# A transformer block on one core: phi's block matrix spread on chip, folds on 120 rows throughout, two folds in idle banks, modulation loaded ahead of the second x tile

## The chip, the core and the metric

The kernel runs on one core of a Trainium2 chip. A core has five engines with a queue of instructions each: TensorE (PE in the profile, with its weight loads as PEld), VectorE (DVE), ScalarE (ACT), GpSimd (POOL) and SyncE (SP), which here issues transfers. They share an on-chip memory of 128 partitions (SBUF), and PE writes its products into eight banks of a second one (PSUM). The metric is the device time of one execution in microseconds (us); three runs were taken and their median counts.

## The reference, cut to what matters

The input x has 2048 tokens of 640 features. All is 32-bit floating point.

```
mod = silu(c) @ w_mod                      # six rows of 640: sa, ca, ga, sb, cb, gb
h = layernorm(x) * (1 + ca) + sa
q, k, v = h @ wqkv                         # 32 heads of 20
pq, pk = q @ w_phi, k @ w_phi              # per head, 20x20
phi = concat(softmax(p), softmax(-p))      # per head
kv = phi_k^T v;  z = sum_s phi_k
o = (phi_q kv) / (phi_q z + 1e-6)
x = x + ga * (o @ wo)
h = layernorm(x) * (1 + cb) + sb
x = x + gb * (relu(h @ w1 + b1)^2 @ w2 + b2)
```

## The kernel before, in words

Tokens go in 16 tiles of 128, loaded two at a time (x0, x1 and so on: `load_x(j)`). A matrix product of full precision is made from three fast ones: each operand is split into a high part (ScalarE copies it to the type fp32r) and a low part (VectorE subtracts, `lo`, line 88). So most operands cost one step on ScalarE and one on VectorE after they are made.

The change lies in the prologue, up to the first tiles. Its work is this:

- *Warm-up.* `WARM` products of a tile of ones (line 563) run before any data has landed.
- *Folds.* Since phi is linear per head, w_phi is multiplied into the K and Q weights once. `fold(nm, d)` (line 246) makes one of five 128-row chunks: six products, five with 120 columns (six heads of 20 each) and one with 40 (the last two heads). The stationary operand is a piece of the raw weights, transposed on the host, with the six heads' 120 features on the partitions; the moving one is a slice of `bd_t`, the block matrix of w_phi with 640 columns, zero off the blocks. The last group has two heads, so its operands have 40 rows. The result lies in a pair of PSUM banks (`pj`, tag "pj": four banks, so two pairs that folds use in turn), from which `split` copies it out, two halves on ScalarE and two on VectorE.
- *Statistics.* `stats` (line 495) takes the mean and variance of an x tile on VectorE and a power on GpSimd; `scale` (line 511) normalizes both token tiles on ScalarE.
- *Modulation.* `mod_rows2(d)` (line 520) multiplies silu(c) with one fifth of the columns for sa and ca (`wm`), `mod_sb` copies the result to SBUF (`msb`, ScalarE), `mod_cols2` transposes it (line 538) and sums it into columns on VectorE (`cols_a`). `out0` then scales the transposed x by these columns into `hT` and splits it. The transposed x lies in halves of the three banks `kvp`, which are otherwise first used later, for phi_k^T v.
- *First K products.* `k_step(d)` adds chunk d to the K products of both token tiles (`pk`), which fill all four "pj" banks over five steps. `to_sb` copies them out (`k`), and `do_q` then starts the Q products (`pq`) in the same banks.
- *V weights.* `v_hi` and `v_lo` split the raw V weights (`rawv` to `wv`).

In this part the order on all five engines is that of the code (`manual_schedule` from line 195). SP issues all loads from one queue in the order of the code. After it a scheduler, and then orders by hand, set the rest: for all tile pairs K, V, Q, phi and the sums over tokens; then the normalized outputs, `wo` and the second layer norm; then the two large products of the last layers (`up` and `acc`), some two fifths of the chain of waits.

## Time and profile before

| | |
|---|---|
| median of 3 runs | 802.65 us (800.93 to 805.67) |
| profiled execution: span | 799.8 us; its own device time is not on the page |
| median run less that span | 2.85 us |
| PE busy | 786.2 us (98%) |
| VectorE, ScalarE busy | 580.0 us (73%), 443.7 us (55%) |
| start of the first fold | 6.43 us |
| start of the first product with Q weights (pq) | 39.46 us |

Times in the profile are us from the first instruction, durations of single instructions ns. In a row of the order of time stand start, duration, engine, line, operation, tiles as out<-in, shape and count; in brackets how long the engine had been idle and what released it. Rows of equal instructions that follow each other are merged. PE's ends are modelled, since products overlap: the spacing of starts tells more than durations. A product of 32-bit operands is two passes and counts twice.

### The profile page before, as it was taken

Reading aid. Unit: us, or ns where it says so; the run is one execution under the profiler, and the core shown is the slowest. Engines: PE = TensorE matmul, PEld = TensorE weight load, DVE = VectorE, ACT = ScalarE, POOL = GpSimd, SP = SyncE. Lnnn points to the kernel's source line nnn. Section 1 sums busy time; section 2 is a strip of 40 time slices with the busy share of each in tenths; the row PEclk is TensorE's granted clock in tenths of the full one; section 3 lists DMA queues with packets and bytes.
Section 4 is the critical chain, followed back from the end, with each engine's and each line's share of the span. In section 5 each row is a group of like instructions: output and inputs, shape, how many; then the busy total and the mean of one; then the engine's idle time right before and its main releaser. Section 6 shows DMA issues by size and latency. Waiting matters only on the chain.

```text
span 799.8 us, 15255 instructions
## 1 busy us (share of the span) xinstructions
PE 786.2 (98%) x5983; PEld 750.7 (94%) x5983; DVE 580.0 (73%) x1046; ACT 443.7 (55%) x988; POOL 127.8 (16%) x259
## 2 busy tenths in 40 slices
PE   9999999999999999999999999999999999999997
PEld 8899999999999878898899999989999999999997
DVE  4499889999788688993546666765857566675756
ACT  4667675576753355555777736455454545536431
POOL 3001021010000114331100000121131313212110
PEclk9999999999999999999999999999999999999999
DMA  9713326423120243321347355896575848557360
GB/s 330 289 35 128 115 83 203 148 84 116 67 100 1 80 168 132 116 83 67 116 150 240 122 197 210 283 302 220 181 215 171 252 145 268 168 184 225 104 187 34
DMA packets 50816, 126.30 MB, mean 158 GB/s; under 512 B 5872, under 2 KB 7152, under 8 KB 50744
## 3 DMA queue, kind: packets, MB, share of 16 engines
q1 hardware_dynamic: 33688, 84.32, 30.8%
q0 software_dynamic: 14752, 35.76, 15.3%
q10 hardware_dynamic: 2304, 5.24, 1.7%
q8 instruction: 47, 0.77, 0.4%
q14 instruction: 25, 0.20, 0.1%
HBM read 95.32 MB, written 29.88 MB: 157 GB/s over the span
## 4 chain that ended last, share of the span: by engine, by line
PE 80%; DVE 9%; ACT 4%; DMA 3%; POOL 2%; issue 1%; ACTq 0%; POOLq 0%; DVEq 0%
PE up L78 20%; PE acc L78 15%; PE pk L78 8%; PE pq L78 7%; PE pv L78 7%; PE pwo L78 7%; PE acc3x L78 4%; PE kvp L421 2%; DMA ring_c<-td_c 2%; DVE dn L790 2%; DVE scr L788 2%; PE te L829 2%; DMA ring_a<-td_a 1%; PE tb L340 1%; PE ta L340 1%
## 5 line engine op out<-in xcount | busy, mean ns | idle before, releaser
L78 PE MATMUL up<-h,w 128*128 128x256 f32 x1640 | 208.9, 279 | 0.4 <-ACT ft L1149 0.4
L78 PEld LDWEIGHTS up<-h,w 128*128 128x128 f32 x1640 | 197.8, 188 | 2.0 <-ACT ft L1149 1.8
L1149 ACT ACTIVATE ft<-up,b_t 128x256 f32<-128x256 f32 x104 | 49.0, 471 | 111.0 <-PE up L78 110.6
L78 PE MATMUL acc<-w,ra 128*128 128x384 f32 x452 | 98.7, 337 | 0.2
L78 PE MATMUL pwo<-wo,ot 128*128 128x256 f32 (+3 forms) x512 | 83.1, 315 | 0.1
L1150 DVE TENSOR_TENSOR ft<-ft 128x256 f32<-128x256 f32 x104 | 44.0, 423 | 52.9 <-ACT ft L1149 52.1
L78 PE MATMUL pk<-wk,hT 128*128 128x384 f32 (+1 forms) x480 | 77.3, 312 | 0.9 <-ACT hT L352 0.9
L78 PEld LDWEIGHTS pwo<-wo,ot 128*128 128x128 f32 (+1 forms) x512 | 75.7, 188 | 1.9 <-ACT ot L866 0.4
L78 PEld LDWEIGHTS acc<-w,ra 128*128 128x128 f32 x452 | 73.0, 188 | 2.8 <-DVE ra L88 1.7
L78 PE MATMUL pq<-wq,hT 128*128 128x384 f32 (+1 forms) x480 | 75.0, 311 | 0.4 <-ACT k L397 0.4
L78 PE MATMUL pv<-wv,hT 128*128 128x384 f32 (+1 forms) x480 | 75.2, 309 | 0.0
L78 PEld LDWEIGHTS pk<-wk,hT 128*128 128x128 f32 x480 | 71.7, 188 | 2.7 <-ACT hT L352 1.1
L78 PEld LDWEIGHTS pq<-wq,hT 128*128 128x128 f32 x480 | 70.7, 188 | 1.5 <-ACT k L397 0.9
L78 PEld LDWEIGHTS pv<-wv,hT 128*128 128x128 f32 x480 | 70.6, 188 | 0.4
L88 DVE TENSOR_TENSOR ra<-ft,ra 128x384 fp32r<-128x384 f32 (+2 forms) x86 | 36.8, 449 | 30.9 <-ACT ra L1173 17.6
L88 DVE TENSOR_TENSOR h<-hfb,h 128x256 fp32r<-128x256 f32 x40 | 17.0, 425 | 48.1 <-ACT h L352 48.0
L1173 ACT ACTIVATE ra<-ft 128x384 fp32r<-128x384 f32 x48 | 25.2, 526 | 29.2 <-DVE ft L1150 28.0
L78 PE MATMUL acc3x<-w,ra 128*128 128x256 f32 x248 | 41.3, 279 | 0.0
L1255 POOL DMA_DIRECT2D ring_c<-td_c x34 | 18.5, 544 | 139.4 <-PE acc L78 113.1
L78 PEld LDWEIGHTS acc3x<-w,ra 128*128 128x128 f32 x248 | 38.4, 188 | 0.4 <-DVE y L1312 0.2
L792 POOL TENSOR_TENSOR dn<-dn,rs_q 128x64 f32<-128x64 f32 x16 | 14.0, 875 | 128.0 <-DVE dn L790 128.0
L1164 DVE TENSOR_TENSOR ft<-ft 128x128 f32<-128x128 f32 x136 | 33.3, 286 | 1.2
(241 smaller groups left out, 1424.2 us busy)
## 6 DMA issues: line engine op xcount, KB each, us to landing
ring_c<-td_c POOLq DMA_DIRECT2D x34, 384.0 KB, 4.1
ring_a<-td_a POOLq DMA_DIRECT2D x34, 384.0 KB, 4.9
ring_b<-td_b POOLq DMA_DIRECT2D x34, 256.0 KB, 3.5
esp<-eq SPq DMA_DIRECT2D x12, 640.0 KB, 2.9
el<-esp SPq DMA_DIRECT2D x12, 640.0 KB, 3.9
rw<-in_w SPq DMA_DIRECT2D x23, 320.0 KB, 3.8
wm<-in_w_mod SPq DMA_DIRECT2D x20, 320.0 KB, 4.0
xb<-in_x SPq DMA_DIRECT2D x8, 640.0 KB, 4.0
```

Of the source, the lines that this page charges most:

```text
L78: nc.tensor.matmul(o, a, b, start=first and i == 0, stop=last and i == len(terms) - 1, skip_group_check=skip,)
L88: (eng or nc.vector).tensor_tensor(out_lo, full, hi.bitcast(F32), op=ALU.subtract)
L340: nc.tensor.transpose(p[:, i * P : (i + 1) * P], xn[:, i, d * P : (d + 1) * P], ident)
L421: nc.tensor.matmul(kvp[64 * c : 64 * c + 64, g // 4, a : a + 2 * n].rearrange("p (s n) -> p s n", s=2), v[:, u], e[:, :, o : o + n], start ...
L788: nc.vector.tensor_tensor(z, flat(ET[t]), flat(zb), op=ALU.mult)
L790: nc.vector.tensor_reduce(dn.rearrange("p s h -> p (s h)"), heads(z), axis=AX.X, op=ALU.add)
L829: nc.tensor.transpose(p[:m, a : a + P], EU[2 * j + i][:, b : b + m], ident)
L1149: nc.scalar.activation(r, p, AF.Relu, bias=b1_t[:, f : f + 1])
L1150: nc.vector.tensor_tensor(r, r, r, op=ALU.mult)
L1164: nc.vector.tensor_tensor(t[:, o], t[:, a], t[:, b], op=op)
L1173: nc.scalar.activation(a[:, 0, :3], t[:, :3], AF.Copy)
L1255: nc.gpsimd.dma_start(RING[j, n, r], TD[n][r].bitcast(F32R))
```

## The change

Six things, all in the prologue:

- `WARM` is 11 in place of 14.
- The host passes w_phi as 120x120 values (56 KB, all blocks side by side by their place within a group) in place of the 128x640 matrix (320 KB). On chip, GpSimd makes a 120x6 pattern of ones (`own`, a memset and two selects), and VectorE multiplies the two, spread over each other, into `bd_t` (two instructions). This stands ahead of VectorE's other work.
- The last group of every fold has 120 rows too. Its 80 more rows of raw weights are set to zero by a VectorE memset, before the load of the 40 real rows, which moves behind the first chunk's load. `bd_t` is zero there.
- The folds of Q chunks 0 and 3 write to two banks of `kvp` (`side_banks`) in place of a "pj" pair.
- The five loads of modulation weights go out together, ahead of the second x tile's. The modulation products of chunks 3 and 4 are made together, a step earlier, and their transposes too.
- The statistics of x1 and its scaling each move one step of `k_step` back; four K folds and not three stand ahead of x0's statistics, and two Q folds ahead of its scaling.

On PE, from the last product of the K folds through the first Q folds, before (foldk and foldq with 0 and 1 are the two banks of a "pj" pair):

```order
L256 MATMUL foldk_1_302<-bd_t,raw_k_129 128x40
L256 MATMUL foldq_0_316<-bd_t,raw_q_138 128x120 x3
L256 MATMUL foldq_1_317<-bd_t,raw_q_138 128x120 x2
L256 MATMUL foldq_1_317<-bd_t,raw_q_140 128x40
L256 MATMUL foldq_0_329<-bd_t,raw_q_138 128x120 x3
```

and after:

```order
L275 MATMUL foldk_1_307<-bd_t,raw_k_133 128x40
L275 MATMUL kvp<-bd_t,raw_q_143 128x120 x5
L275 MATMUL kvp<-bd_t,raw_q_145 128x40
L275 MATMUL foldq_0_330<-bd_t,raw_q_143 128x120 x3
L275 MATMUL foldq_1_331<-bd_t,raw_q_143 128x120 x2
```

The first Q fold goes to kvp's banks, and the second takes the pair that the first had.

On PE, around the last Q fold, before (kvp<-ident,xb are transposes of x, kvp<-ident,msb those of the modulation, mrow its products):

```order
L538 MATMUL kvp<-ident,msb_369 128x128
L256 MATMUL foldq_0_387<-bd_t,raw_q_140 128x120 x3
L256 MATMUL foldq_1_388<-bd_t,raw_q_140 128x120 x2
L256 MATMUL foldq_1_388<-bd_t,raw_q_140 128x40
L527 MATMUL mrow_399<-wm_149,cs 32x128 x10
L340 MATMUL kvp<-ident,xb_136 128x128 x6
L538 MATMUL kvp<-ident,msb_414 128x128
L527 MATMUL mrow_434<-wm_153,cs 32x128 x10
```

and after:

```order
L548 MATMUL mrow_364<-wm_153,cs 32x128 x10
L359 MATMUL kvp<-ident,xb_141 128x128 x2
L275 MATMUL foldq_0_384<-bd_t,raw_q_145 128x120 x3
L275 MATMUL foldq_1_385<-bd_t,raw_q_145 128x120 x2
L275 MATMUL foldq_1_385<-bd_t,raw_q_145 128x40
L561 MATMUL kvp<-ident,msb_381 128x128
L548 MATMUL mrow_398<-wm_155,cs 32x128 x10
L359 MATMUL kvp<-ident,xb_141 128x128 x8
L561 MATMUL kvp<-ident,msb_413 128x128
L548 MATMUL mrow_435<-wm_157,cs 32x128 x10
```

The first modulation transpose stands behind the fifth Q fold now, and only two transposes of x stand ahead of that fold, eight behind it.

On ScalarE, around the scaling of x1 (xb<-xb), before:

```order
L351 ACTIVATE hfa_3_506<-kvp,cols_a 128x256
L352 ACTIVATE hT_216<-hfa_3_506 128x256
L534 ACTIVATE msb_533<-mrow_510,plus 128x128
L513 ACTIVATE xb_151<-xb_151,nba_493,sqa_492 128x640 x2
L351 ACTIVATE hfa_4_539<-kvp,cols_a 128x256
L352 ACTIVATE hT_216<-hfa_4_539 128x256
L605 ACTIVATE wv_567<-rawv_159 128x640
L397 ACTIVATE k_570<-pk_0_424 128x384
```

and after:

```order
L370 ACTIVATE hfa_3_507<-kvp,cols_a 128x256
L371 ACTIVATE hT_224<-hfa_3_507 128x256
L370 ACTIVATE hfa_4_537<-kvp,cols_a 128x256
L371 ACTIVATE hT_224<-hfa_4_537 128x256
L532 ACTIVATE xb_163<-xb_163,nba_526,sqa_525 128x640 x2
L627 ACTIVATE wv_567<-rawv_165 128x640
L416 ACTIVATE k_570<-pk_0_425 128x384
L416 ACTIVATE k_570<-pk_1_426 128x256
```

The scaling has moved behind the last hT and stands directly ahead of the V weights and the copies of pk. On VectorE x1's statistics stand behind the fourth hT's low part, where they stood behind the third's.

The diff, cut:

```diff
...
-WARM = 14
+WARM = 11
...
 
     ones = const.tile([P, P], F32, name="ones")
     nc.gpsimd.memset(ones, 1.0)
+
+    bdc = row("s3", "bdc")
+    own = bdc[:120, P : P + 6]
+    nc.gpsimd.memset(own, 1.0)
+    nc.gpsimd.affine_select(out=own, in_=own, compare_op=ALU.is_ge, fill=0.0, base=0,
+                            pattern=[[-DH, 6]], channel_multiplier=1)
+    nc.gpsimd.affine_select(out=own, in_=own, compare_op=ALU.is_ge, fill=0.0, base=DH - 1,
+                            pattern=[[DH, 6]], channel_multiplier=-1)
     ident = const.tile([P, P], F32, name="ident")
     make_identity(nc, ident)
     neg = const.tile([P, P], F32R, name="neg")
...
     first.__enter__()
 
     nc.sync.dma_start(c_t, c)
+    nc.sync.dma_start(bdc[:120, :120], bd)
     bd_t = row("s4", "bd_t")
-    nc.sync.dma_start(bd_t, bd)
     raw, WM, RV, XB = {}, {}, {}, {}
 
     def load_raw(nm, w5, w1):
         raw[nm] = [tok2("w", f"raw_{nm}{i}") for i in range(3)]
-        nc.sync.dma_start(raw[nm][2][:40, 1], w1)
+        nc.vector.memset(raw[nm][2][:, 1], 0.0)
         for d in range(NC):
             nc.sync.dma_start(raw[nm][d // 2][:, d % 2], w5[d * P : (d + 1) * P])
+            if d == 0:
+                nc.sync.dma_start(raw[nm][2][:40, 1], w1)
 
     def load_x(j):
         XB[j] = tok2(f"x{j % 2}", f"xb{j}")
...
     load_raw("k", wk5, wk1)
     load_x(0)
     load_raw("q", wq5, wq1)
-    for d in range(2):
+    for d in range(NC):
         load_wm(d)
     load_x(1)
-    for d in range(2, NC):
-        load_wm(d)
     for d in range(NC):
         if d % 2 == 0:
             both = tok2("w", f"rawv{d}")
         RV[d] = both[:, d % 2]
         nc.sync.dma_start(RV[d], wv[d * P : (d + 1) * P])
+
+    by_head = bdc[:120, :120].rearrange("p (g f) -> p g f", f=DH)
+    nc.vector.tensor_tensor(
+        bd_t[:120, :600].rearrange("p (g i f) -> p g i f", i=6, f=DH),
+        by_head[:, :5, None, :].to_broadcast([120, 5, 6, DH]),
+        own[:, None, :, None].to_broadcast([120, 5, 6, DH]), op=ALU.mult
+    )
+    nc.vector.tensor_tensor(
+        bd_t[:120, 600:].rearrange("p (i f) -> p i f", f=DH),
+        by_head[:, 5:6, :].to_broadcast([120, 2, DH]), over(own[:, :2]), op=ALU.mult
+    )
 
     cs = const.tile([P, NC], F32, name="cs")
     ce = const.tile([P, NC], F32, name="ce")
...
 
     W = {}
 
-    def fold(nm, d):
+    def fold(nm, d, p=None):
 
         w = wslot(f"w{nm}{d}")
         W[nm, d] = w
-        p = pj(f"fold{nm}{d}")
+        p = p or pj(f"fold{nm}{d}")
         for g, (o, n) in enumerate(GR):
             if g < 5:
-                r = raw[nm][d // 2][:n, d % 2, g * P : (g + 1) * P]
+                r = raw[nm][d // 2][:120, d % 2, g * P : (g + 1) * P]
             else:
-                r = raw[nm][2][:n, 1, d * P : (d + 1) * P]
+                r = raw[nm][2][:120, 1, d * P : (d + 1) * P]
             nc.tensor.matmul(
-                p[g // 3][:, (g % 3) * 120 : (g % 3) * 120 + n], r, bd_t[:n, g * 120 : g * 120 + n],
+                p[g // 3][:, (g % 3) * 120 : (g % 3) * 120 + n], r, bd_t[:120, g * 120 : g * 120 + n],
                 start=True, stop=True,
             )
 
...
 
     MR = {}
 
-    def mod_rows2(d):
-
-        MR[d] = tp(f"mrow{d}")
-        for k in range(NC):
-            for s in range(2):
-                c = 2 * (k % 2) + s
-                a = 256 * k + P * s
-                nc.tensor.matmul(
-                    MR[d][32 * c : 32 * c + 32, :P], cs[:, k : k + 1].to_broadcast([P, 32]), WM[d][:, a : a + P],
-                    start=(k < 2), stop=(k >= NC - 2), skip_group_check=True,
-                )
-
...
+    def mod_rows2(*ds):
+
+        p = tp(f"mrow{ds[0]}")
+        for m, d in enumerate(ds):
+            MR[d] = p[:, m * P : m * P + P]
+            for k in range(NC):
+                for s in range(2):
+                    c = 2 * (k % 2) + s
+                    a = 256 * k + P * s
+                    nc.tensor.matmul(
+                        MR[d][32 * c : 32 * c + 32], cs[:, k : k + 1].to_broadcast([P, 32]), WM[d][:, a : a + P],
+                        start=(k < 2 and m == 0), stop=(k >= NC - 2), skip_group_check=True,
+                    )
+
...
 
     TR = [half(0, 0), half(1, 0), half(1, 1), half(2, 0), half(2, 1)]
     mem.tile([P, 48], F32, tag="gap", name="gap", bufs=1)
...
     def out0(d):
         t_out(cols_a, HT[0], d, "a0", TR[d])
 
+    side_banks = [kvp[:, 1], kvp[:, 2]]
     warm = tp("warm")
     for i in range(WARM):
         nc.tensor.matmul(warm[:, :P], ones, ones, start=True, stop=True)
-    for d in range(3):
+    for d in range(4):
         fold("k", d)()
     n0 = stats(XB[0], "a0")
-    for d in range(3, NC):
-        fold("k", d)()
+    fold("k", 4)()
+    fold("q", 0, side_banks)()
+    fold("q", 1)()
     scale(XB[0], *n0)
-    for d in range(2):
-        fold("q", d)()
+    fold("q", 2)()
+    split = fold("q", 3, side_banks)
+    mod_rows2(0)
     t_in(XB[0], 0, TR[0])
-    t_in(XB[0], 1, TR[1])
-    fold("q", 2)()
-    mod_rows2(0)
+    split()
     mod_sb(0)
-    split = fold("q", 3)
+    split = fold("q", 4)
     mod_cols2(0)
-    split()
-    split = fold("q", 4)
     out0(0)
     mod_rows2(1)
     split()
     mod_sb(1)
-    for d in range(2, NC):
+    for d in range(1, NC):
         t_in(XB[0], d, TR[d])
     load_x(2)
     PP += [pj(f"pk{t}") for t in range(2)]
+    rows_at, cols_at = {0: (2,), 1: (3, 4)}, {0: (1,), 1: (2,), 2: (3, 4)}
     for d in range(NC):
+        mod_cols2(*cols_at.get(d, ()))
         if d + 1 < NC:
-            mod_cols2(d + 1)
             out0(d + 1)
-        if d + 2 < NC:
-            mod_rows2(d + 2)
+        if d in rows_at:
+            mod_rows2(*rows_at[d])
         k_step(d)
-        if d + 2 < NC:
-            mod_sb(d + 2)
-        if d == 1:
+        mod_sb(*rows_at.get(d, ()))
+        if d == 2:
             n1 = stats(XB[1], "a1")
-        if d == 2:
+        if d == 3:
             scale(XB[1], *n1)
 
     def v_hi(d):
...
 
     A_x, A_wqkv, A_w_phi, A_wo = (np.asarray(a) for a in (A_x, A_wqkv, A_w_phi, A_wo))
     B_w1, B_b1, B_w2, B_b2, c, w_mod = (np.asarray(a) for a in (B_w1, B_b1, B_w2, B_b2, c, w_mod))
-    bd = np.zeros((P, D), A_w_phi.dtype)
+    bd = np.zeros((6, DH, 6, DH), A_w_phi.dtype)
     for h in range(H):
-        i = h % 6
-        bd[i * DH : (i + 1) * DH, h * DH : (h + 1) * DH] = A_w_phi[h]
+        bd[h % 6, :, h // 6] = A_w_phi[h]
     b1 = np.zeros((NF * P,), B_b1.dtype)
     b1[:F] = B_b1
     b1[F:] = B_b1[F - FS[-1] :]
...
```

More of the change, by code (lines that the diff above doesn't have):

```diff
@@ L518, with mod_sb, mod_cols2 @@
     MR = {}
-    def mod_rows2(d):
-        MR[d] = tp(f"mrow{d}")
-        for k in range(NC):
-            for s in range(2):
-                c = 2 * (k % 2) + s
-                a = 256 * k + P * s
-                nc.tensor.matmul(
-                    MR[d][32 * c : 32 * c + 32, :P], cs[:, k : k + 1].to_broadcast([P, 32]), WM[d][:, a : a + P],
-                    start=(k < 2), stop=(k >= NC - 2), skip_group_check=True,
-                )
-    def mod_sb(d):
-        t = MR[d, "sb"] = row("s1", f"msb{d}")[:, :P]
-        nc.scalar.activation(t, MR[d][:, :P], AF.Identity, bias=plus[:, 0:1])
-    def mod_cols2(d):
-        p = half(0, 1)[:, P * (d % 2) : P * (d % 2) + P]
-        nc.tensor.transpose(p, MR[d, "sb"], ident)
-        nc.vector.tensor_reduce(
-            cols_a.rearrange("p (s d) -> p s d", s=2)[:, :, d],
-            p.rearrange("p (h s r) -> p s h r", h=2, s=2)[:, :, :, 0], axis=AX.X, op=ALU.add,
-        )
+    def mod_rows2(*ds):
[10 more added lines that the diff above has]
+                    )
+    def mod_sb(*ds):
+        for d in ds:
+            t = MR[d, "sb"] = row("s1", f"msb{d}")[:, :P]
+            nc.scalar.activation(t, MR[d], AF.Identity, bias=plus[:, 0:1])
+    def mod_cols2(*ds):
+        for d in ds:
+            p = half(0, 1)[:, P * (d % 2) : P * (d % 2) + P]
+            nc.tensor.transpose(p, MR[d, "sb"], ident)
+            nc.vector.tensor_reduce(
+                cols_a.rearrange("p (s d) -> p s d", s=2)[:, :, d],
+                p.rearrange("p (h s r) -> p s h r", h=2, s=2)[:, :, :, 0], axis=AX.X, op=ALU.add,
+            )
     TR = [half(0, 0), half(1, 0), half(1, 1), half(2, 0), half(2, 1)]
```

2 lines of the change are left out of this document (1 added, 1 removed).

## The prediction

> **What bounds the kernel now.** I read the page, then the chain of waits over the first 70 us, the same stretch in order of time, the groups by shape, and the landings. An effect under 0.5% (4 us) is about what a measurement of this kernel cannot tell from no change.
>
> ```profile
> span 799.8 us, 15255 instructions
> PE 786.2 (98%) x5983; PEld 750.7 (94%) x5983; DVE 580.0 (73%) x1046; ACT 443.7 (55%) x988; POOL 127.8 (16%) x259
> ```
>
> TensorE (PE) is busy for 98% of the span, so an edit counts by what it does to the line of work on PE. Behind the prologue every engine keeps its instructions and their order. So I sum up to the first product with the Q weights (pq) and take the rest as shifted. Pieces of the chain there (start, duration):
>
> ```profile
> 24.63 0.78 PE mrow L527 x20
> 25.41 0.81 PE kvp L340 x6
> 26.22 0.11 PE kvp L538
> 27.11 1.92 PE pk L78 x12
> 39.62 4.31 PE pq L78 x30
> ```
>
> **Warm-up and folds.** The first two rows are the warm-up before and after about 5.6 us; then folds, the copies behind them, weight loads by shape, and two loads that waited.
>
> ```profile
> 1.05 4.76 PE L563 MATMUL warm<-ones 128*128 128x128 f32 x21 [1.05 <-POOL ones L147]
> L563 PE MATMUL warm<-ones x8: 274/275/337, 5.5 to 6.3; 128*128 128x128 f32 x8
> 6.43 1.92 PE L256 MATMUL foldk<-bd_t,raw_k 120*128 120x120 f32 x13
> 8.19 0.97 PEld L256 LDWEIGHTS foldk<-bd_t,raw_k 120*128 120x128 f32 x8
> 8.94 0.47 ACT L263 ACTIVATE wk<-foldk 128x360 fp32r<-128x360 f32 x1 [0.45 <-PE foldk L256]
> 10.59 0.47 ACT L263 ACTIVATE wk<-foldk 128x360 fp32r<-128x360 f32 x1 [0.45 <-PE foldk L256]
> L256 PEld LDWEIGHTS foldk<-bd_t,raw_k 120*128 120x128 f32 x50 | 6.0, 191 | 0.2
> L256 PEld LDWEIGHTS foldk<-bd_t,raw_k 40*128 40x128 f32 x10 | 1.5, 184 | 0.6
> 14.74 3.25 PEld L256 LDWEIGHTS foldq<-bd_t,raw_q 120*128 120x128 f32 x24 [0.23 <-DVE wk L88]
> 18.78 1.60 PEld L256 LDWEIGHTS foldq<-bd_t,raw_q 120*128 120x128 f32 x12 [0.32 <-DVE wq L88]
> ```
>
> Each f32 product is two passes. The early warm passes start (4.76 - 0.34) / 20 = 0.22 us apart. Eight fold loads of 120 rows start (0.97 - 0.19) / 7 = 0.111 us apart. Three warm products fewer take away six of the late passes: 6 x 0.111 = **-0.67**, so the first fold may start at 6.43 - 0.67 = 5.76.
>
> A fold is 12 passes, 1.33 us at that spacing, yet the copies show one fold in 10.59 - 8.94 = 1.65 us. What differs inside a fold is the pair of passes on 40 rows, and the loads idle ahead of those (0.6 us over 10, against 0.2 over 50). I put the missing 0.31 us to going from 120 rows to 40 and back. With 120 rows throughout, ten folds give **-3.1**. The bounds are 0 (the pair costs this whatever its rows are) and that; I take the latter, since the 120-row passes are the nearest row.
>
> The Trainium skill ("TensorE: Matmul & The Clock Gate", LDWEIGHTS) says that a load takes a time that goes by its columns, however many rows it has. The trace agrees, with 184 ns against 191. By that rule alone the change of rows gains nothing, and the sum would be 3.1 us higher.
>
> Two Q folds in kvp's idle banks end the two waits for a bank pair in the last two rows: **-0.55**. ScalarE and VectorE need under 1.1 us a fold, less than 1.33.
>
> **What the first fold waits for.** The new wait is for phi's matrix from VectorE. Issues, landings (issue to landing), two windows (the last column is what DMA moved, in GB/s), and the nearest multiplication:
>
> ```profile
> 0.80 0.40 SPq L198 DMA_DIRECT2D c_t<-in_c  x1
> 1.25 0.42 SPq L200 DMA_DIRECT2D bd_t<-in_bd  x1
> c_t<-in_c SPq DMA_DIRECT2D x1, 2.5 KB, 1.6
> DMA to landing us min/median/max: 5.3/5.8/6.3
> 2.00:4.00 2.00, 2.00 (x12) 2.00 (x11) 0.53 (x3) 0.59 (x3) 1.84 (x13) 1.00 0.82 183
> 4.00:6.00 2.00, 2.00 (x13) 2.00 (x13) 0.00 (x0) 0.00 (x0) 1.63 (x9) 1.00 0.99 292
> L404 DVE TENSOR_TENSOR ek<-k,mxk 128x640 f32<-128x640 f32 x2 | 1.6, 822 | 0.0
> ```
>
> The compact block (56 KB for 320) is issued where bd_t was, at 1.25. Its landing lies between 1.6 us later (c_t's) and 5.3 (the soonest K weight, the fourth row): 2.85 to 6.55. The spread is one multiplication of 600 columns and one of 40, together about the 0.82 of the last row and 0.2 for the second start, so bd_t is ready between 3.9 and 7.6. By bytes, 60 KB have moved well before 4.0 at 183 GB/s. It is the next in the queue behind c_t, so I take a landing near that end, 3.8, and a ready matrix at 4.8. The first K chunk now has 0.39 MB up to its end, where it had 0.76: about 4.1 instead of 5.35 at those rates. It was used at 6.43, so the landing lags the bytes by at most 1.1, and it is there by 5.2. Both lie under 5.76, so I add nothing; the upper end, 7.6, is a rival.
>
> The two memsets of the padding rows on VectorE (128x640, under 0.82 each) end before the block lands, where VectorE had nothing. GpSimd's memset and two selects for the pattern of ones delay masks that are needed much later. SP issues as many transfers as before, and only the first padding memset can hold it.
>
> **Modulation and the second x tile.** The next rows are the chain from the first modulation product to the second (msb), then the work around x1's statistics.
>
> ```profile
> 22.85 0.33 PE L538 MATMUL kvp<-ident,msb 128*128 128x128 f32 x1
> 23.42 0.56 ACT L351 ACTIVATE hfa<-kvp,cols_a 128x256 f32<-128x256 f32 x1
> 24.34 0.75 ACT L263 ACTIVATE wq<-foldq 128x360 fp32r<-128x360 f32 x2
> 25.46 0.37 ACT L534 ACTIVATE msb<-mrow,plus 128x128 f32<-128x128 f32 x1 [0.37 <-PE mrow L527]
> 28.87 0.27 PE L538 MATMUL kvp<-ident,msb 128*128 128x128 f32 x1
> 30.77 0.88 DVE L503 BATCH_NORM_STATS2 sta<-xb 128x6 f32<-128x320 f32 x2
> 34.82 1.74 ACT L513 ACTIVATE xb<-xb,nba,sqa 128x640 f32<-128x640 f32 x2 [0.60 <-POOL nba L508]
> 36.46 0.55 ACT L351 ACTIVATE hfa<-kvp,cols_a 128x256 f32<-128x256 f32 x1
> 37.36 0.72 ACT L605 ACTIVATE wv<-rawv 128x640 fp32r<-128x640 f32 x1
> 37.51 2.11 PE L78 MATMUL pk<-wk,hT 128*128 128x384 f32 x12 [0.90 <-ACT hT L352]
> 38.45 1.63 ACT L397 ACTIVATE k<-pk 128x384 f32<-128x384 f32 x4 [0.36 <-PE pk L78]
> 39.46 4.47 PE L78 MATMUL pq<-wq,hT 128*128 128x384 f32 x30
> 12.35 0.44 SPq L211 DMA_DIRECT2D xb<-in_x  x1
> xb<-in_x SPq DMA_DIRECT2D x4, 640.0 KB, 7.5
> ```
>
> Today PE waits 0.90 us for the last hT, since ScalarE scales x1 first. The change sets hT ahead of the scaling, **-0.90**, but the scaling then stands ahead of the copies that empty the banks of pk, and pq needs those banks.
>
> I walk PE through the new order. From 5.76, nine folds of 1.33 end at 17.73. One modulation product (0.78), two transposes (0.27) and the tenth fold end at 20.11. The chain from a transposed msb to the next msb takes on ScalarE (23.42 - 22.85) + (24.34 + 0.75 - 23.42) + 0.37 = 2.61, so msb is there at 22.72. PE meanwhile does 0.11, a product (0.78) and eight transposes (1.08), and is at 22.08: it waits **+0.64**. Then 0.11, 0.78, the first pk step 1.92, 0.11, two products 1.56 and the second pk step bring it to 29.12. Two transposes and three steps of 1.92 end at 35.10.
>
> VectorE starts x1's statistics 30.77 - 28.87 = 1.90 after the transposed msb, plus 0.1 for a second one: 31.12. The scaling follows 34.82 - 30.77 = 4.05 later, at 35.17. It holds ScalarE for 36.46 - 34.82 = 1.64, the V weights' first half for 0.72, and the first copy of pk for 0.49 (the four take 1.63). So pq starts at 38.0, and PE has waited **+2.9**. Before, it started at 39.46: a gain of 1.45.
>
> x1 landed at 12.35 + 7.5 = 19.85. It moves behind three loads of 640 KB, at 292 GB/s 6.7 us more, so by 26.6, before 31.1. PE's gain is VectorE's loss: its first spread starts 0.5 to 1 us sooner, not 1.45, and this work was done some us ahead of its users.
>
> **Sum.** -0.67 - 3.1 - 0.55 - 0.90 + 0.64 + 2.9 = -1.7; the walk gives -1.45, as it keeps small starts. The profiled span goes from 799.8 to 798.35. The median run, 802.65, is 2.85 above that span (the page has no other time for the execution), so 801.2.
>
> **The rivals.**
> - *The clock falls in the new wait.* At the start PE needed 4.4 us at 0.22 a pass until it ran at 0.111. If 2.9 us of idling bring that back, 20 passes cost 2.2 more: 803.4. Against it: the 0.90 wait shown had pk and pq at their usual pace behind it. The same page of the Trainium skill (the HAM clock gate) has the clock fall after an idle window of about 3.4 us; the wait stays under that, and no row here has one as long.
> - *The rows gain nothing* (columns alone count, and the pair's cost is something else): +3.1, 804.3.
> - *phi's matrix is late.* This ends on the slow side: with the landing at the K weights' 5.3 us, bd_t is ready at 7.6 and the folds start 1.84 late: 803.0. It decides from a first fold at 5.76 + 1.45 = 7.21. Against it: it is second in the queue, at a sixth of the bytes.
> - *The wait before pq does not come,* because the copies get in earlier: 801.2 - 2.9 = 798.3. Against it: the order on ScalarE is fixed.
>
> **How the numbers follow.** Forecast 0.58, clock 0.09, rows 0.08, late matrix 0.10, no wait 0.07, others 0.08. The time is the likeliest's, 801.2. The range goes from 799.2 (2.0 of the wait of 2.9 hidden) to 803.6, which takes in the late matrix and the clock. Only a missing wait reaches 0.5% faster (below 798.6), and slower by that much needs something unnamed above 806.7: 0.07 faster, 0.87 within, 0.06 slower.
>
> **What would show it.** In the changed kernel: a first fold near 5.8; copies of wk 1.33 apart; all fold loads 120 rows without idle time; PE idle for 2.5 to 3 us ahead of pq, ended by ScalarE's copy of k; pq near 38.0. A first fold after 7.2, folds still 1.65 apart, or slow passes behind that wait would make the forecast wrong, each by the price above.

## The result, and the profile after

The changed kernel takes 802.36 us (median of 14 runs, 799.13 to 806.77), the kernel before 802.53 (14 runs beside them, 799.71 to 805.67). The ratio is 1.0004, with a 95% interval from 0.9990 to 1.0018: no difference that this measurement can tell. The forecast was 801.2, within 0.5%. The profiled execution of the changed kernel took 801.59 us, 1.69 more than its span.

The page of the changed kernel, its span and its engines:

```profile
span 799.9 us, 15251 instructions
PE 781.9 (98%) x5977; PEld 747.7 (93%) x5977; DVE 582.1 (73%) x1050; ACT 443.1 (55%) x988; POOL 127.9 (16%) x262
```

PE is 4.3 us less busy than before (786.2), yet the span is 0.1 longer: what PE no longer does, it now waits. The same kernel in order of time, PE alone up to pq (start, duration; in brackets the idle time ahead and what ended it). These are all the rows with a wait, and the first fold:

```profile
1.05 4.30 PE L587 MATMUL warm<-ones 128*128 128x128 f32 x22 [1.05 <-POOL bdc L151]
5.19 1.43 PE L275 MATMUL foldk<-bd_t,raw_k 120*128 120x120 f32 x12
7.42 5.55 PE L275 MATMUL foldk<-bd_t,raw_k 120*128 120x120 f32 x48 [0.80 <-DMA raw_k<-in_wk]
21.63 0.30 PE L561 MATMUL kvp<-ident,msb 128*128 128x128 f32 x1 [0.88 <-DVE wq L88]
24.14 0.33 PE L561 MATMUL kvp<-ident,msb 128*128 128x128 f32 x1 [0.27 <-ACT msb L556]
31.11 0.30 PE L561 MATMUL kvp<-ident,msb 128*128 128x128 f32 x1 [0.35 <-DVE cols_a L562]
35.49 1.65 PE L78 MATMUL pk<-wk,hT 128*128 128x384 f32 x10 [0.27 <-DVE hT L88]
39.73 4.58 PE L78 MATMUL pq<-wq,hT 128*128 128x384 f32 x30 [2.58 <-ACT k L416]
```

The first Q fold starts at 12.80, so the four K folds behind the wait take (12.80 - 7.42) / 4 = 1.345 us each, as forecast (1.33). But there are six waits, of 5.15 us together, and pq starts at 39.73 where it started at 39.46: the folds' gain is gone before the first Q product. The last wait is the largest. Its cause on ScalarE, in order of time:

```profile
36.94 1.73 ACT L532 ACTIVATE xb<-xb,nba,sqa 128x640 f32<-128x640 f32 x2 [3.38 <-POOL nba L527]
39.20 1.39 ACT L416 ACTIVATE k<-pk 128x384 f32<-128x384 f32 x4
```

ScalarE began to scale x1 just 0.2 us before pk was complete (35.49 + 1.65 = 37.14). The four copies that free its banks stand behind that scaling (1.73) and the split of the first V weight. VectorE's spread of phi's matrix, on the other hand, is done by 4.35:

```profile
4.12 0.23 DVE L248 TENSOR_TENSOR bd_t<-bdc 120x40 f32<-120x40 f32 x1
```

From pq to the end both take nearly the same time (799.8 - 39.46 = 760.3, 799.9 - 39.73 = 760.2), so what is to be explained lies ahead of it, and in what the runs beside this profile did. That the two agree to 0.1 us is in part luck: over the eleven profiled executions of this document in which the clock stayed full while PE had work, this stretch took 758.8 to 762.4 us. A span of one execution can't show less than that; the start of pq and the medians can.

### The profile page after: what moved, and what is told of

Its sections match the earlier page's. It is cut to its first block, busy times and chain, and to the rows that moved or that the text cites. A ratio compares the mean times of both kernels' runs of the same rounds, so it can differ in the third digit from the quotient of the medians.

```text
span 799.9 us, 15251 instructions
## 1 busy us (share of the span) xinstructions
PE 781.9 (98%) x5977; PEld 747.7 (93%) x5977; DVE 582.1 (73%) x1050; ACT 443.1 (55%) x988; POOL 127.9 (16%) x262
## 4 chain that ended last, share of the span: by engine, by line
PE 79%; DVE 8%; DMA 5%; ACT 4%; POOL 2%; issue 1%; SPq 0%; ACTq 0%; POOLq 0%
PE up L78 20%; PE acc L78 15%; PE pk L78 8%; PE pq L78 7%; PE pv L78 7%; PE pwo L78 7%; PE acc3x L78 5%; DMA ring_c<-td_c 4%; PE kvp L440 2%; DVE dn L812 2%; DVE scr L810 2%; PE te L851 2%; PE tb L359 1%; PE ta L359 1%; DVE ezb L831 1%
```

## The experiments

The theory after this reading: PE's line up to pq decides; the change gave about 5 us there (less work on PE, and the waits of the kernel before gone) and took them back by new waits, half of them the one before pq. The rivals: the gain is given back behind pq by VectorE; the rows gave nothing; the clock falls in the new wait.

Times are device medians; ratios go to the kernel before, run on the same chip in the same group (its medians: 802.13, 803.89 and 801.99 in the three groups).

### 1. Scale x1 behind the copies

```
-        if d == 3:
-            scale(XB[1], *n1)
...
         to_sb(PP[t], PK[t])
+    scale(XB[1], *n1)
     for d in range(1, NC):
         v_hi(d)
```

> The changed kernel with one thing moved: ScalarE scales the second x tile behind the four copies that empty pk's banks, instead of ahead of them. Theory (what stands on PE's line before pq counts one for one to the end): the wait of 2.58 us before pq shrinks to one copy and its signal, 0.4 to 0.6; pq starts at 37.5 to 37.8 instead of 39.73, and the span is 797.6 to 798.0 instead of 799.9. Rival A (the gain is given back behind pq, because VectorE is the next to be late): pq at 37.5 to 37.8, but the span stays within 0.5 of 799.9. Rival B (pk's banks are held by something else, such as the split of the first V weight): pq stays within 0.5 of 39.73.

798.27 us, ratio 0.9956 (0.9939 to 0.9973), span 796.6. ScalarE and PE of this run, in order of time:

```profile
36.28 1.65 ACT L416 ACTIVATE k<-pk 128x384 f32<-128x384 f32 x4 [1.78 <-PE pk L78]
37.32 4.47 PE L78 MATMUL pq<-wq,hT 128*128 128x384 f32 x30
```

The copies now wait for PE, not PE for them; the wait is gone, pq starts 2.41 sooner, and the span is 3.3 shorter. Rival A and rival B both fall. But the median fell by 4.1 (3.9 by the ratios), more than pq moved. That was not expected, and experiments 4 to 6 take it up. Of the span's 3.3, the 0.9 behind pq lie within the spread of that stretch.

### 2. The last group back on 40 rows

```
...
-                r = raw[nm][2][:120, 1, d * P : (d + 1) * P]
+                r = raw[nm][2][:n, 1, d * P : (d + 1) * P]
...
-                p[g // 3][:, (g % 3) * 120 : (g % 3) * 120 + n], r, bd_t[:120, g * 120 : g * 120 + n],
+                p[g // 3][:, (g % 3) * 120 : (g % 3) * 120 + n], r, bd_t[:n, g * 120 : g * 120 + n],
```

> The changed kernel with the last group of each fold back on 40 rows, all else kept. Theory (going from 120 rows to 40 and back costs 0.31 us a fold): copies of wk 1.64 to 1.66 apart instead of 1.34; the wait for the second K chunk (0.80) shrinks by 0.3, so PE is 2.5 to 2.8 later behind the folds, and pq starts near 42.3, the span is near 802.5. Rival (the number of rows costs nothing, the shorter pitch comes from the matrix being written by VectorE, or from the earlier clock): copies 1.34 apart, pq near 39.7, span 799.9.

804.44 us, ratio 1.0039 (1.0020 to 1.0057), span 802.7. Two of the copies behind folds, and pq:

```profile
8.85 0.47 ACT L282 ACTIVATE wk<-foldk 128x360 fp32r<-128x360 f32 x1 [0.46 <-PE foldk L275]
10.49 0.47 ACT L282 ACTIVATE wk<-foldk 128x360 fp32r<-128x360 f32 x1 [0.45 <-PE foldk L275]
42.51 4.58 PE L78 MATMUL pq<-wq,hT 128*128 128x384 f32 x30 [2.57 <-ACT k L416]
```

The folds are 10.49 - 8.85 = 1.64 apart again, pq is 2.78 later, the span 2.8 longer. The rows are the cause of the pitch, and the folds count nearly one for one: the wait before pq stays (2.57), because x1's statistics follow PE's work and move along with it (on VectorE they start 1.6 us behind the second column sum in both traces). That pq moved by just 2.78 is in part luck: in this execution the first fold started 0.71 later (5.90), the wait of 0.80 for the second K chunk did not come, and the wait of 0.88 was 0.69. The rule of the Trainium skill that was weighed in the prediction ("TensorE: Matmul & The Clock Gate", LDWEIGHTS: a load's time goes by columns) holds for the loads themselves: those of 40 rows took 184 ns here, those of 120 rows for the Q folds 191. By it alone there would have been no difference in the pitch.

### 3. The rows alone

The kernel before, with the operands of `fold` on 120 rows as in the diff of the change (not shown again), and what these need:

```
-        nc.sync.dma_start(raw[nm][2][:40, 1], w1)
+        nc.vector.memset(raw[nm][2][:, 1], 0.0)
         for d in range(NC):
             nc.sync.dma_start(raw[nm][d // 2][:, d % 2], w5[d * P : (d + 1) * P])
+            if d == 0:
+                nc.sync.dma_start(raw[nm][2][:40, 1], w1)
```

> The kernel before with only the rows changed: the last group of each fold on 120 rows with memsets of the padding, phi's full matrix loaded as before, warm-up of 14, no idle banks, order of modulation as before. Theory (rows alone give the fold pitch): copies of wk 1.34 apart instead of 1.65, and the folds give 2.5 to 3.1 less, because the second K chunk may be late by up to 0.6; pq starts at 36.4 to 37.1 instead of 39.46, the span is 796.8 to 797.5 instead of 799.8: better than the whole change. Rival A (the gain on PE is eaten by a wait behind x1's scaling, as in the whole change): pq within 0.7 of 39.46. Rival B (rows cost nothing): copies 1.65 apart, pq 39.5.

800.93 us, ratio 0.9982 (0.9962 to 1.0001), span 799.4. PE's waits in the folds, the last pk step and pq:

```profile
14.08 2.87 PE L258 MATMUL foldq<-bd_t,raw_q 120*128 120x120 f32 x24 [0.72 <-DVE wk L88]
18.11 1.53 PE L258 MATMUL foldq<-bd_t,raw_q 120*128 120x120 f32 x12 [0.37 <-DVE wq L88]
36.20 2.13 PE L78 MATMUL pk<-wk,hT 128*128 128x384 f32 x12 [0.93 <-ACT hT L354]
38.18 4.47 PE L78 MATMUL pq<-wq,hT 128*128 128x384 f32 x30
```

pq is 1.28 sooner, not 2.4 to 3.1: between the theory and rival A. With folds at 1.34, VectorE, which also does x0's statistics there, leaves a bank pair late (0.72, where the wait was 0.23), and the wait for x1's scaling (0.93) is as before. Even so, this one part starts pq sooner than the whole change does (38.18 against 39.73).

### 4. The first modulation product ahead of the split

```
+    mod_sb(0)
     t_in(XB[0], 0, TR[0])
+    mod_cols2(0)
     split()
-    mod_sb(0)
     split = fold("q", 4)
-    mod_cols2(0)
     out0(0)
```

> The changed kernel with the first modulation product copied out and transposed ahead of the split of the fourth Q fold, instead of behind it. Theory (the 0.88 us that PE waits ahead of the first transposed product come from VectorE and ScalarE taking the halves of that fold in turn): that wait falls to 0.2 or less, the next one (0.27) goes, pq starts at 38.6 to 39.0 instead of 39.73, span 798.8 to 799.2. Rival (x1's statistics and scaling hold pq whatever PE does earlier): the wait goes, but the one before pq grows from 2.58 to about 3.5, pq stays at 39.7.

802.64 us, ratio 1.0006 (0.9988 to 1.0024), span 801.6. PE:

```profile
19.78 0.33 PE L561 MATMUL kvp<-ident,msb 128*128 128x128 f32 x1
22.95 1.09 PE L359 MATMUL kvp<-ident,xb 128*128 128x128 f32 x8 [0.79 <-ACT hfa L370]
39.87 5.96 PE L78 MATMUL pq<-wq,hT 128*128 128x384 f32 x30 [2.55 <-ACT k L416]
```

The wait of 0.88 is gone and stands, as 0.79, ahead of the next transposes, so neither theory had it right: what PE waited for was the state of kvp as a whole (experiment 7). The third row is the surprise: the first thirty Q products took 5.96 us instead of 4.58. The stretches around it (PE's busy time, the granted clock, DMA):

```profile
38.00:39.00 1.00, 0.00 (x0) 1.00 0.00 0
39.00:40.00 1.00, 0.13 (x1) 0.67 0.00 0
40.00:41.00 1.00, 1.00 (x4) 0.50 0.00 0
41.00:42.00 1.00, 1.00 (x5) 0.50 0.06 16
42.00:43.00 1.00, 1.00 (x5) 0.62 0.00 0
```

In this execution the clock fell to half in the wait of 2.55 us, at 39.35, and stayed there for 3.41 us, to 42.76. In the profiled execution of the changed kernel the same wait (2.58) left it at 1.0.

### 5. Dummy products in the wait

```
+    keep = tp("keep")
+    for i in range(11):
+        nc.tensor.matmul(keep[:, :P], ones, ones, start=True, stop=True)
     do_q(0)
```

> The changed kernel with eleven products of ones by ones, into a bank that nobody reads, put on PE between the last pk product and pq. They take 11 x 0.22 = 2.4 us, where PE otherwise stands idle for 2.58; no other engine's order changes. Theory (in most executions the clock falls behind that wait, as the run with the first modulation ahead of the split showed: pq took 5.96 there instead of 4.58): PE no longer idles long, the mean granted clock of nearly all runs is 0.998 or more (the changed kernel: 10 of 14 at 0.997 or less), and the median falls by 1.0 to 1.5 to 800.9 to 801.4. Rival (the wait itself is all there is, clocks differ by chance): the median stays at 802.0 to 802.8 and the clocks at 0.996 to 0.997. The profiled execution has pq at 39.5 to 40.3 either way.

801.78 us, ratio 0.9971 (0.9957 to 0.9986). PE:

```profile
37.48 2.62 PE L650 MATMUL keep<-ones 128*128 128x128 f32 x22
40.23 4.58 PE L78 MATMUL pq<-wq,hT 128*128 128x384 f32 x30
```

Every one of the 12 runs has a mean clock of 0.998 or more, against 4 of 14 of the changed kernel. One fall of 3.41 us takes 0.002 off the mean. The clock also falls in the last microseconds, when PE is done (that alone took the profiled execution of experiment 10 to 0.998). So 0.997 or less shows a fall on the way, while 0.998 does not rule one out. With that caution the falls belong to the idle time. How much of the median it is remains less clear: by ratio the dummies gain 2.6 us on the changed kernel, by plain medians 0.6, since the kernel before ran slower in this group (803.89).

### 6. Half as many dummies

```
-    for i in range(11):
+    for i in range(5):
```

> The changed kernel with five products of ones ahead of pq instead of eleven, so that PE idles 2.58 - 5 x 0.22 = 1.4 us there in place of 2.58. Theory (the clock falls only behind an idle stretch of about 2.5 us): pq at the same place, at its usual 4.5 to 4.6; nearly all clocks at 0.998 or more, as with eleven. Rival (the clock goes by how much of a stretch of time PE was idle, so 1.4 us is enough in some executions): 3 or more of 12 runs at 0.997 or less.

801.72 us, ratio 1.0000 (0.9982 to 1.0017). PE:

```profile
36.03 1.28 PE L650 MATMUL keep<-ones 128*128 128x128 f32 x10
38.76 4.66 PE L78 MATMUL pq<-wq,hT 128*128 128x384 f32 x30 [1.45 <-ACT k L416]
```

11 of 12 runs have 0.998 or more: 1.45 us of idling is not enough. The count is the one that the theory said. The ratio, though, is that of the changed kernel, not that of eleven dummies, so by these two runs the fall's share of the median is somewhere from nothing to 2.6 us. The mean granted clock of the timed runs, with the longest idle stretch of PE between the first fold and pq in the profiled execution (experiments by number):

```
kernel                     idle us    runs at 0.997 or less
changed                    2.58       10 of 14
40 rows (2)                2.57        5 of 12
msb first (4)              2.55       10 of 12
three tiles (7)            2.47        4 of 12
c behind K (12)            2.02        9 of 12
dummies, five (6)          1.45        1 of 12
rows alone (3)             0.93        0 of 12
scaling moved (1)          0.88        1 of 12
dummies, eleven (5)        0.87        0 of 12
warm-up of 14 (9)          0.87        1 of 12
no idle banks (10)         0.72        1 of 9
full matrix (11)           0.54        1 of 7
all waits (8)              0.41        3 of 6
before, three groups       0.90        2 of 35, 7 of 29, 2 of 27
```

The last but one has its fall elsewhere (experiment 8), and such falls, behind other waits, are likely what the few low runs of the others and of the kernel before are; no trace shows those. Within the changed kernel, the ten runs at 0.997 or less have a median of 802.8 and the other four 801.2. An estimate from the price of one fall on pq (1.4 in experiment 4, 1.6 in experiment 7) and these ten of fourteen gives the falls about 1 us of the median.

The clock records of the traces show why the same wait brings a fall or not. In each of the fourteen profiled executions they change only at moments that lie a whole number of 3.413 us apart: 5.21 (full clock), 39.35 and 42.76 in experiment 4; 4.37, 38.50 and 41.91 in experiment 7; 6.89, 532.54 and 535.96 in experiment 8. Where this grid lies differs from one execution to the next. With each execution cut into such windows, the clock fell at the end of every window in which PE had idled 2.03 us or more (2.03, 2.47 and 2.43 in these three; 2.25 and more when PE was done), and of none with 1.75 or less. In the changed kernel a window ended at 38.53, in the middle of the wait. It parted the idle time into 1.66 us (with the 0.27 ahead of it) and 1.19, and the clock stayed.

So experiment 6's rival had the mechanism, idling as a share of a stretch of time; only its 1.4 us are too little. An estimate for a grid that lies anywhere with equal chance: a wait of 2.58 puts that much into one window in 57% to 73% of the executions, (3.41 + 2.58 - 2 x 2.03) / 3.41 to (3.41 + 2.58 - 2 x 1.75) / 3.41, and a wait of 1.45 in none. The table has 10 of 14, 29 of 50 over the four kernels with waits of 2.47 to 2.58, and 1 of 12.

### 7. kvp as three tiles

```
-    kvp = psK.tile([P, 3, 512], F32, name="kvp")
+    kvp = [psK.tile([P, 512], F32, name=f"kvp{b}") for b in range(3)]
```

(and the places that index it).

> The changed kernel with kvp declared as three tiles of one bank instead of one tile of three; banks, work and order stay. Theory (the 0.88 us ahead of the first transposed modulation product are waits that the program sets because all three banks are one tile: ScalarE's copy of a fold's second half waits for VectorE's work on the first, and PE's write to the first bank waits for VectorE's reading of the second): the wait falls from 0.88 to 0.1 to 0.3; the next one grows from 0.27 to about 0.5, as ScalarE's line behind it (two copies for hT, two of the split, msb) is what it is; from the first Q fold to pq it is 0.4 to 0.8 less. Rival (the engines really get in each other's way in PSUM): copies get longer and the waits stay. The wait before pq stays at 2.5 to 2.6, so the median is 801.5 to 802.3.

800.69 us, ratio 0.9964 (0.9945 to 0.9983), span 801.4. First the lockstep in the changed kernel, in order of time, then PE of this run:

```profile
19.52 0.47 ACT L282 ACTIVATE wq<-kvp 128x360 fp32r<-128x360 f32 x1 [0.38 <-PE kvp L359]
20.02 0.53 DVE L88 TENSOR_TENSOR wq<-kvp,wq 128x360 fp32r<-128x360 f32 x1 [0.26 <-ACT wq L282]
20.59 0.40 ACT L282 ACTIVATE wq<-kvp 128x280 fp32r<-128x280 f32 x1 [0.60 <-DVE wq L88]
21.03 0.45 DVE L88 TENSOR_TENSOR wq<-kvp,wq 128x280 fp32r<-128x280 f32 x1 [0.47 <-ACT wq L282]
```

```profile
7.63 5.81 PE L275 MATMUL foldk<-bd_t,raw_k 120*128 120x120 f32 x48 [1.02 <-DMA raw_k<-in_wk]
21.04 0.30 PE L561 MATMUL kvp<-ident,msb 128*128 128x128 f32 x1
38.48 6.14 PE L78 MATMUL pq<-wq,hT 128*128 128x384 f32 x30 [2.47 <-ACT k L416]
```

ScalarE had waited for VectorE on another bank, and PE for both, only because the program orders its accesses by tile; with three tiles ScalarE's two copies follow each other without a wait and are no longer than before, so the rival falls. With three tiles the 0.88 is gone and so is the 0.27 ahead of the last pk step. From the first Q fold (13.27 here, 12.80 there) to pq it is 25.21 instead of 26.93, 1.72 less where 0.4 to 0.8 was expected: about 1.06 of it ahead of the first transposed product and 0.67 behind the last one. The clock fell here as well: pq took 6.14. So the median still holds some of these falls (4 of 12 runs).

### 8. All these waits taken away

Three tiles; the scaling of experiment 1; x1's statistics behind the last hT; and in `mod_cols2` both transposes of a pair ahead of both sums:

```
...
         for d in ds:
             nc.tensor.transpose(p[d], MR[d, "sb"], ident)
+        for d in ds:
             nc.vector.tensor_reduce(
...
-        if d == 2:
+        if d == 3:
             n1 = stats(XB[1], "a1")
...
```

> The changed kernel with the waits that it made taken away together: kvp as three tiles; the transposes of the last two modulation products both ahead of their column sums; x1's statistics behind the last hT instead of ahead of it; x1's scaling behind the copies of pk. Theory (each counts one for one, and each was measured in the trace of the changed kernel or of the run with the scaling moved): against that run (pq at 37.32, span 796.6) another 0.65 + 0.35 + 0.26 = 1.26 less; pq at 36.0 to 36.5 with the clock's step where it was there, span 795.2 to 795.8, median 796.9 to 797.4. Rival (VectorE takes over: the statistics now stand ahead of its work on k, so spread starts later and something behind pq waits): pq as forecast, span 796.3 or more.

796.98 us (6 runs), ratio 0.9906 (0.9881 to 0.9931), span 796.5: below both kernels, with its interval clear of theirs. PE up to pq, and one row of a later stage:

```profile
29.64 0.38 PE L561 MATMUL kvp<-ident,msb 128*128 128x128 f32 x2
29.78 5.43 PE L78 MATMUL pk<-wk,hT 128*128 128x384 f32 x36
35.04 4.47 PE L78 MATMUL pq<-wq,hT 128*128 128x384 f32 x30
532.21 1.06 PE L78 MATMUL acc<-ring_c,ra 128*128 128x384 f32 x3 [2.43 <-DMA ring_c<-td_c]
```

pq starts at 35.04, a further 2.3 us sooner than in experiment 1, where 0.8 to 1.3 was expected: 4.4 before the kernel before. The span followed less far in this execution, because PE waited 2.43 us for a transfer at 529.8, and the granted clock was 0.50 from 532.54 to 535.96.

### 9. Three warm-up products put back

On top of experiment 1:

```
-WARM = 11
+WARM = 14
```

> The run with x1's scaling moved, with the three warm-up products put back (14). Theory (the three products count 6 x 0.111 us, as the landing of K's second chunk rarely holds the folds): the first fold and pq are 0.5 to 0.7 later at an equal step of the clock, the median 798.8 to 799.1 instead of 798.27. Rival (what is taken off the warm-up is waited for at the K weights, as in the profiled execution of the changed kernel, 0.80): median within 0.3 of 798.27.

800.52 us, ratio 0.9961 (0.9944 to 0.9977), against 0.9956 without them. Warm-up and first folds of both, those without them first:

```profile
1.05 5.07 PE L587 MATMUL warm<-ones 128*128 128x128 f32 x22 [1.05 <-POOL bdc L151]
5.91 7.39 PE L275 MATMUL foldk<-bd_t,raw_k 120*128 120x120 f32 x60
```

```profile
1.05 5.23 PE L587 MATMUL warm<-ones 128*128 128x128 f32 x28 [1.05 <-POOL bdc L151]
6.11 7.00 PE L275 MATMUL foldk<-bd_t,raw_k 120*128 120x120 f32 x60
```

22 passes took 5.07 us and 28 took 5.23: PE reached its full pace sooner in the second execution, and its K folds even ended sooner (13.11 against 13.30). The step to full pace moves by more than the term of 0.67 from one execution to the next: the fourteen profiles have it between 4.1 and 7.2 us. The term is neither shown nor refuted.

### 10. No idle banks

On top of experiment 1:

```
-    fold("q", 0, side_banks)()
+    fold("q", 0)()
...
-    split = fold("q", 3, side_banks)
+    split = fold("q", 3)
```

> The run with x1's scaling moved, with the first and the fourth Q fold back in the rotating bank pairs instead of kvp's idle banks. Theory (the idle banks are worth what the folds otherwise wait for a pair, but they cost the 0.88 us ahead of the first transposed modulation product, since kvp is one tile): waits of 0.2 to 0.7 come ahead of the Q folds, 1.0 to 1.4 in all (0.72 + 0.37 stood there in the kernel before on 120 rows), and the wait ahead of the first transposed product falls to 0.3 or less; from the first Q fold to pq it is 0.2 to 0.6 longer than in the run compared (24.02). Rival (ScalarE and VectorE keep up with folds of 1.34 us, as the prediction had it, and the idle banks gain nothing): no bank waits over 0.3, and that stretch is 0.5 to 0.9 shorter.

798.34 us, ratio 0.9952 (0.9936 to 0.9968). PE:

```profile
12.64 1.51 PE L275 MATMUL foldq<-bd_t,raw_q 120*128 120x120 f32 x12
14.87 4.21 PE L275 MATMUL foldq<-bd_t,raw_q 120*128 120x120 f32 x36 [0.72 <-DVE wk L88]
21.33 0.30 PE L561 MATMUL kvp<-ident,msb 128*128 128x128 f32 x1
36.70 4.47 PE L78 MATMUL pq<-wq,hT 128*128 128x384 f32 x30
```

A bank wait of 0.72 comes, the 0.88 goes. The stretch from the first Q fold's start to pq's is 24.06, against 37.32 - 13.13 = 24.19 with the idle banks: as built, they gain nothing. The theory had 0.2 to 0.6 longer, the rival 0.5 to 0.9 shorter; neither. (The 24.02 of the expectation counts from the end of the K folds, 13.30.)

### 11. phi's full matrix

On top of experiment 8, with the two multiplications that spread the matrix left out and the host's matrix as in the kernel before:

```
-    nc.sync.dma_start(bdc[:120, :120], bd)
     bd_t = row("s4", "bd_t")
+    nc.sync.dma_start(bd_t, bd)
...
```

> The run with all waits taken away, with phi's full block matrix loaded (320 KB) as in the kernel before, instead of the compact block spread by VectorE. Theory (the K weights land by bytes, and the folds are now so early that they wait for them): 264 KB more ahead of them at 290 GB/s make each K chunk 0.9 later; the first fold waits until 6.0 to 6.6 and the second or the later ones wait too, 0.4 to 1.0 in all; pq at 35.5 to 36.1 instead of 35.04. Rival (phi's matrix and the chunks are there anyway, and the compact block gains nothing): no waits for K weights over 0.1, pq within 0.3 of 35.04.

796.3 us (7 runs), ratio 0.9941 (0.9920 to 0.9963). PE:

```profile
6.31 1.50 PE L264 MATMUL foldk<-bd_t,raw_k 120*128 120x120 f32 x12 [0.50 <-DMA raw_k<-in_wk]
8.35 5.55 PE L264 MATMUL foldk<-bd_t,raw_k 120*128 120x120 f32 x48 [0.54 <-DMA raw_k<-in_wk]
35.77 4.47 PE L78 MATMUL pq<-wq,hT 128*128 128x384 f32 x30
```

As the theory had it: two waits of 1.04 us for K weights, pq 0.73 later. So the compact block is worth some 0.7 us on PE's line here, roughly, since the two executions reached full pace at 6.9 and 5.4 us; the medians can't tell the two kernels apart.

### 12. The load of c behind the K weights

On top of experiment 8:

```
-    nc.sync.dma_start(c_t, c)
     nc.sync.dma_start(bdc[:120, :120], bd)
...
+    nc.sync.dma_start(c_t, c)
     load_x(0)
```

> The run with all waits taken away, with the small load of c issued behind the K weights instead of first. Theory (SP issues one transfer in 0.42 to 0.46, so phi's block and the first K chunks are issued and land 0.4 sooner): the first fold can start as soon as the warm-up ends in every execution, and the second chunk is not waited for; pq 0 to 0.4 sooner, median 0 to 0.4 below that of the run compared by its ratio. Rival (what lands by bytes lands no sooner): no difference beyond the step of the clock, which moved the first fold between 5.2 and 5.9.

800.04 us, ratio 0.9976 (0.9963 to 0.9990): worse than experiment 8 by 3.1 us in plain medians and by 5.6 by the ratios, and pq starts 2.29 later (37.33). ScalarE and PE:

```profile
9.70 0.21 ACT L256 ACTIVATE ce<-c_t 128x5 f32<-128x5 f32 x1 [7.63 <-DMA c_t<-in_c]
11.23 4.21 PE L275 MATMUL foldk<-bd_t,raw_k 120*128 120x120 f32 x36 [2.02 <-DVE wk L88]
```

Both expectations missed it: ScalarE and VectorE have the work on c at the head of their queues, ahead of the copies that empty the folds' banks. They stood until c landed, and the third fold waited 2.02 us for a bank pair. How soon the K weights land without c can't be read from this run. 9 of its 12 runs have a clock of 0.997 or less; the profiled one kept its clock, with the wait parted by a window's end at 10.43, so no trace shows that it is this wait.

## Why the prediction was right, and where it was not

The time came out right (801.2 against 802.36, in the range), and so did the forecast of no clear difference. The walk to pq, however, was 1.73 short (38.0 against 39.73), and the span 1.55 (798.35 against 799.9). That the time is nearer than the walk is luck: the median lay 2.46 us over the profiled span, where 2.85 was carried over. Only 1.7 of either is what a run takes beyond its own span; the rest says how the profiled execution happened to lie among the others. And some 1 us of the median is falls of the clock, which the sum does not have. Point by point:

- **Folds, -3.1: right.** The pitch of 1.34 is in the trace, and experiment 2 gives 2.78 on pq and 2.8 on the span, in part by its start. The rival that the rows gain nothing falls.
- **Warm-up, -0.67 to a first fold at 5.76: not testable.** The first fold started at 5.19 in the profile, and at 5.07 to 5.91 in the other profiled runs with 11 products and the compact block, as the pace changed. The sum took one moment of the step to full pace for granted; it lay between 4.1 and 7.2 us.
- **phi's matrix: right.** Estimated at 4.8, ready at 4.35; the rival of a late matrix falls.
- **"Both lie under 5.76, so I add nothing": the step that failed first.** It asked whether the matrix and the first K chunk were there, and not whether the second was, which folds that are earlier and faster reach sooner. It came at 7.42: 0.80 us of waiting, 1.02 in experiment 7. (From the forecast start of 5.76 the second fold would have stood there at 7.09 and waited 0.33.) In most other profiles the second chunk was there, but the third was late by 0.24 to 0.40 where the first fold started between 5.58 and 5.73 (experiments 4, 5 and 10); landings move from one execution to the next, and in experiment 6 folds from 5.07 on waited for nothing. Experiment 11 shows that K's landing does carry over to pq.
- **Idle banks, -0.55: as a wait right, as a sum wrong.** The two bank waits went, and a wait of 0.88 came at the first transposed product, through the one tile that holds all three banks. Experiments 7 and 10 show both sides; the net is nothing.
- **The hT wait, -0.90: mis-sized.** 0.27 was left, since x1's statistics stand ahead of the last low part on VectorE.
- **The msb wait, +0.64: mis-sized.** At that place 0.27; with the 0.88 and the 0.35 between the paired transposes, 1.50 in all. The pair's cost was put at 0.1.
- **The wait before pq, +2.9: right.** It is 2.58 and ended by ScalarE's copy of k, and experiment 1 removes it by one move. The rival that it does not come falls.
- **The clock, a chance of 0.09: underrated.** The forecast profile is the one that the page shows, with the clock at 1.0. But in two of the four profiled runs with this wait (the changed kernel, experiments 2, 4 and 7) the clock fell to half, at 1.4 to 1.6 us (5.96 and 6.14 for 4.58; the rival's price was 2.2), and 10 of the changed kernel's 14 runs show low clocks. The argument against it from the length of the wait failed: 2.03 us of idling in one window were enough (experiment 6). Its share of the median is an estimate, about 1 us; the two runs with dummies leave it between nothing and 2.6.

The walk's 1.73 is made up, from the rows above, of 0.54 up to the first modulation product (18.27 against 17.73; the chunk's wait of 0.80, less the 0.57 that the first fold was early, and 0.31 from folds that take a little over 1.33), 0.88 - 0.37 at the two transposed products, 0.35 for the pair, 0.27 at the last pk step, -0.32 at pq, and 0.38 of small starts that the walk left out.

## What to carry to other kernels

A faster stage reaches its next wait sooner: for every wait that is priced at nothing, look at the load or the bank after it, not only at the first. Put the copies that free banks ahead of work on the same engine that nobody awaits yet; moving two instructions took a change that gained nothing to 0.44% below the kernel before. And in this program two uses of different banks of one tile are ordered as if they met (experiment 7), so give each bank its own tile.

## What was not expected of the hardware

- An idle stretch of 2.4 to 2.6 us was enough for the granted clock to fall to 0.50 for 3.41 us: before pq (2.55 and 2.47 us idle) and at 532 us in experiment 8 (2.43). At the same place 2.58 and 2.57 left it at 1.0 in other executions. The Trainium skill ("TensorE: Matmul & The Clock Gate", Part 1) has the clock fall after an idle window of about 3.4 us, of windows that run freely of the kernel. The traces agree with the length and with the free running (experiment 6). They differ on the idling: a window with 2.03 us of it was enough, one with 1.75 was not. So a wait shorter than 1.75 us was safe in these traces, and a longer one was hit or not by where the window's end lay.
- A group of passes on 40 rows among groups on 120 costs PE 0.30 us a fold (1.64 for 1.34), which padding with zeros takes away (experiment 2). Why, and whether it is the change of rows or the 40 rows themselves, no run shows.
- The slow pace at the start (0.22 us a pass) looks as if it were not in the granted clock, which the views give as 1.00 there. But the traces hold no clock record before the step: the first one, full clock, comes at 4.40 us in the changed kernel, where the passes go from 0.21 us apart to 0.11, and so in the other thirteen profiles (4.14 to 7.16).
